# The order of the first loads and of the second pair's preparation in a fused Mamba-2 and feed-forward kernel

## Chip, cores and metric

The kernel runs on one core of one Trainium2 chip. The metric is the device time of one execution in microseconds (us), the median over runs. Matrix products run on TensorE (PE in the profile), elementwise work on VectorE (DVE), ScalarE (ACT) and GpSimd (POOL); SyncE (SP) issues most of the transfers, GpSimd those of the weights, and all transfers are carried out by 16 DMA engines.

## What is computed

The first part is a linear-recurrence attention (Mamba-2 SSD) over 4 batches, 8 heads and 768 positions with head size 32 and state size 16; its result, laid out as 3072 tokens of 256 features, goes through a feed-forward layer with 2048 hidden units and a squared ReLU.

```python
# x (4,8,768,32)  a (4,8,768)  B, C (4,8,768,16)  w_in (256,2048)  w_out (2048,256), all float32
log_a = np.log(np.clip(a, 1e-06, 1.0))
for c in range(nc):                         # chunks of 32 positions, state (N x D) per head
    cum = np.cumsum(la, axis=-1)
    L = np.exp(cum[..., :, None] - cum[..., None, :]) * causal
    CB = np.einsum('bhin,bhjn->bhij', Cc, Bc)
    y_intra = np.einsum('bhij,bhjd->bhid', CB * L, xc)
    y_inter = np.einsum('bhin,bhnd->bhid', Cc, state) * np.exp(cum)[..., None]
    y[:, :, sl] = y_intra + y_inter
    state = decay_full * state + np.sum(Bx * decay_from_j, axis=2)
x2 = y.transpose(0, 2, 1, 3).reshape(3072, 256)
h = np.maximum(x2 @ w_in, 0.0)
out = (h * h) @ w_out
```

## The kernel before

**Tiling.** The 768 positions of a batch are cut into three stretches of 256, which gives 12 pairs (batch, stretch), `PAIRS`, numbered k = 0 to 11 with the four batches first. Each pair is one block of 256 tokens for the feed-forward layer. The kernel uses a chunk length of its own, two chunks u of 128 positions in each pair, and two positions (r = 0, 1) in a partition.

**Attention of one pair.** `ph_load(k)` issues three transfers on SP (for pair 0, B goes by ScalarE's queue): C and B of 128 KB each, in pieces of 128 bytes, and x of 256 KB, in pieces of 256 bytes. With `gate=`, an engine first writes one element of each buffer, so that the transfer can't be issued before that engine has come to this place. `prep_c` scales C by the cumulative decay `P_sb` (tile cz for the first four pairs), `prep_b` casts B to bfloat16 (Bb), `prep_x` multiplies x by the inverse decay `Pinv` (xs). `ph_tr` transposes Bb and cz on TensorE (six matmuls into tile tr), `ph_bct` copies them out of PSUM on VectorE (bct). `ph_mt` multiplies C with B (mt), `ph_mask` applies the causal mask in four parts (mts), `ph_u` forms the state contribution U from Bb and xs, `ph_s` the state (S, z) and `ph_y` the result Y, which is copied to `T[k]`, the transposed input of the feed-forward layer. For pair 0, half of T is copied by ScalarE and half by VectorE.

**Feed-forward layer.** A step is a block and one of eight parts f of 256 hidden units. `mm1` multiplies `w_in_b` with T (tile hps) and ScalarE applies the ReLU (hb); `square` squares it on VectorE (h), but for the first step on GpSimd; `mm2` multiplies with `w_out_b` four steps later (ops). `finish_block` writes the block out.

**Weights.** They are loaded and cast to bfloat16 by GpSimd's queue in slices of 256 KB (as written): `load_wi(f0, f1)` and `load_wo(f0, f1)`, with f counting groups of 128 hidden units. There are four slices of each, and a small `tensor_copy` to the tile `touch` ahead of some of them reads a tile that another engine has to have written; it holds GpSimd, and so the issue behind it, until then. Before, the first slice wi(0:4) waits in this way for the decay input `a_nat` (line 450), and wi(4:8) for Bb of pair 0 (line 491).

**Order.** All engines work through their instructions in the order of the program; the scheduling is by hand (`manual_schedule`). Lines 445 to 523 are the prologue written out one by one: pair 0, and pair 1 up to its transposes. `warm(n, cols)` puts n matmuls on dummy data into TensorE's queue (tile dps). From line 525 on, a list of steps and a table `todo` say what is issued at each step: before the change, step 0 issues xs of pair 1 and the gated loads of pair 2 (`second_x`), step 3 U of pair 1, step 4 its Y and the `late_loads` (three slices of weights behind a touch of pair 1's state, then the gated loads of pair 3). Pair 2 has its transposes at step 9, U at 12 and Y at 14. GpSimd makes cz of pair 2 at step 6 and its xs at step 7. From pair 4 on, a DMA transpose takes the place of the transposes on TensorE.

Of the kernel before, what the change touches and what calls it, by code (L numbers as in the profile page):

```python
# [16 lines left out]
def _fap(base: bass.AP, offset_elems: int, free_dims):  # L17

    ap0 = list(base.ap)[0]
    return bass.AP(tensor=base.tensor, offset=base.offset + offset_elems,  # L20
                   ap=[list(ap0)] + [list(d) for d in free_dims])


def _dap(base: bass.AP, offset_elems: int, dims):

    return bass.AP(tensor=base.tensor, offset=base.offset + offset_elems,
                   ap=[list(d) for d in dims])
# [3 lines left out]
def kernel(  # L31
# [14 lines left out]
    nc = tc.nc  # L46
# [43 lines left out]
    a_nat = const.tile([96, 256], FP32, name="a_nat")  # L90
    a_cl = const.tile([96, 256], FP32, name="a_cl")
    dum = const.tile([128, 256], BF16, name="dum")
    touch = const.tile([128, 1], FP32, name="touch")
# [3 lines left out]
    P_sb = const.tile([128, 2, 96], FP32, name="P_sb")  # L97
# [32 lines left out]
    def load_wi(f0, f1):  # L130
        nc.gpsimd.dma_start(
            out=w_in_b[:, :, f0 * 128:f1 * 128],
            in_=_dap(moe_w_in, f0 * 128, [[2048, 128], [128 * 2048, 2], [1, (f1 - f0) * 128]]))

    def load_wo(f0, f1):
        nc.gpsimd.dma_start(  # L136
            out=w_out_b[:, f0:f1, :],
            in_=moe_w_out[f0 * 128:f1 * 128, :].rearrange("(f p) d -> p f d", p=128))


    live = {}

    def prep_c(k, eng):
        b, j = PAIRS[k]
        if k >= KDT:
            for r in range(2):
                eng.tensor_tensor(  # L147
                    out=_fap(bc[k % 3], r * 384 + 128, [[144, 2], [32, 4], [1, 16]]),
                    in0=_fap(loaded[k]["C"], r * 16, [[128, 2], [32, 4], [1, 16]]),
                    in1=_fap(P_sb, r * 96 + b * 24 + j, [[12, 2], [3, 4], [0, 16]]), op=ALU.mult)  # L150
            return
        czk = cz[k % 3]
        eng.tensor_tensor(
            out=_fap(czk, 0, [[240, 2], [32, 8], [1, 16]]),
            in0=_fap(loaded[k]["C"], 0, [[16, 2], [32, 8], [1, 16]]),
            in1=_fap(P_sb, b * 24 + j, [[96, 2], [3, 8], [0, 16]]), op=ALU.mult)
        live.setdefault(k, {})["cz"] = czk

    def prep_b(k, eng):
        if k >= KDT:  # L160
            Bb = bc[k % 3][:, :, 0, :]
        else:
            Bb = prep.tile([128, 2, 128], BF16, tag="Bb", name=f"Bb{k}")
        for r in range(2):
            bo = _fap(Bb, r * (384 if k >= KDT else 128), [[16, 2], [32, 4], [1, 16]])
            bi = _fap(loaded[k]["B"], r * 16, [[128, 2], [32, 4], [1, 16]])
            if eng is nc.scalar:
                eng.copy(out=bo, in_=bi)
            else:
                eng.tensor_copy(out=bo, in_=bi)  # L170
        live.setdefault(k, {})["Bb"] = Bb

    def prep_x(k, eng):
        b, j = PAIRS[k]
        xs = prep.tile([128, 2, 256], BF16, tag="xs", name=f"xs{k}")
        eng.tensor_tensor(  # L176
            out=_fap(xs, 0, [[256, 2], [32, 8], [1, 32]]),
            in0=_fap(loaded[k]["x"], 0, [[32, 2], [64, 8], [1, 32]]),
            in1=_fap(Pinv, b * 24 + j, [[96, 2], [3, 8], [0, 32]]), op=ALU.mult)
        live.setdefault(k, {})["xs"] = xs  # L180
# [14 lines left out]
    def ph_tr(k, copy=True):  # L195
        v = live[k]
        pool, tag = (ps_o, "ops") if k < 2 else (ps_s, "A")
        tr = pool.tile([128, 2, 3, 128], BF16, tag=tag, name=f"tr{k}",
                       padded_shape=[128, 2, 4, 128] if k < 2 else [128, 4, 4, 128])
        for r in range(2):  # L200
            nc.tensor.transpose(tr[:, r, 0, :], v["Bb"][:, r, :], eye_b)
            for g in range(2):
                nc.tensor.transpose(tr[:, r, 1 + g, :], v["cz"][:, r, 112 * g:112 * g + 128], eye_b)  # L203
        v["tr"] = tr
        if copy:
            ph_bct(k)

    def ph_bct(k):
        bct = big.tile([128, 2, 3, 128], BF16, tag="bct", name=f"bct{k}")
        nc.vector.tensor_copy(out=bct, in_=live[k]["tr"])  # L210
        live[k]["bct"] = bct
# [17 lines left out]
    def ph_mask(k, q, src=None):  # L229
        v = live[k]  # L230
        nc.vector.tensor_tensor(  # L231
            out=v["mts"][:, q], in0=v["mt"][q // 2][:, q % 2] if src is None else src,
            in1=_fap(cb, 128, [[128, 2], [0, 2], [1, 128]]), op=ALU.mult)
# [210 lines left out]
    with tc.manual_schedule():  # L444
# [2 lines left out]
        ph_load(0, "C")  # L447
        ph_load(0, "B", nc.scalar)
        nc.gpsimd.dma_start(out=cb, in_=cb_d.ap())
        nc.gpsimd.tensor_copy(out=touch[0:96], in_=a_nat[:, 0:1])  # L450
        load_wi(0, 4)

        nc.vector.memset(dum, 0.0)  # L453
        nc.vector.memset(zer, 0.0)
# [8 lines left out]
        def idle_tile():  # L463
            idle.append(ps_o.tile([128, 256], FP32, tag="ops", name=f"dps{len(idle)}", padded_shape=[128, 512]))
# [3 lines left out]
        def warm(n, cols=256):  # L468
            for _ in range(n):
                nc.tensor.matmul(idle[-1][:, 0:cols], dum[:, 0:128], dum[:, 0:cols],  # L470
                                 start=True, stop=True, skip_group_check=True)
# [16 lines left out]
        nc.scalar.copy(out=Ptot, in_=pps)  # L488
        prep_c(0, nc.vector)
        nc.vector.reciprocal(out=_fap(Pinv, 0, [[96, 2], [3, 32]]), in_=_fap(P_sb, 0, [[96, 2], [3, 32]]))  # L490
        nc.gpsimd.tensor_copy(out=touch, in_=live[0]["Bb"][:, 1, 0:1])
        load_wi(4, 8)
        prep_x(0, nc.gpsimd)
        warm(2, 128)
        ph_tr(0)
        warm(8, 128)
# [2 lines left out]
        mtc = big.tile([128, 2, 2, 2, 128], BF16, tag="mtc", name="mtc", bufs=1)  # L499
        for i in (1, 0):  # L500
            nc.scalar.copy(out=mtc[:, i], in_=live[0]["mt"][1][:, i])
        ph_mask(0, 0)
        nc.gpsimd.tensor_copy(out=touch, in_=live[0]["mts"][:, 0, 0, 0, 0:1])
        load_wo(0, 4)
        prep_b(1, nc.gpsimd)
        load_wo(4, 8)
        load_wi(8, 12)
        nc.gpsimd.tensor_tensor(out=Pown, in0=_fap(Ptot, 0, [[1, 24], [0, 4]]),
                                in1=_fap(cb, 384, [[0, 24], [1, 4]]), op=ALU.mult)
        warm(4, 128)  # L510
        ph_u(0)
        warm(12, 128)
        ph_mask(0, 1)
        ph_mask(0, 3, mtc[:, 1])
        ph_mask(0, 2, mtc[:, 0])
        ph_s(0, (0,))
        prep_c(1, nc.vector)
        ph_y(0)
        ph_tr(1, copy=False)
        idle_tile()  # L520
        warm(5, 128)
        ph_bct(1)
        ph_s(0, (1,), "z")

        steps = ([(0, f) for f in range(4)] + [(1, f) for f in range(4)]
# [4 lines left out]
        def at(s, fn, *args):  # L530
            todo.setdefault(max(s, 0), []).append((fn, args))
# [1 line left out]
        def recip_rest(j):  # L533
            nc.vector.reciprocal(out=_fap(Pinv, j, [[96, 2], [3, 32]]), in_=_fap(P_sb, j, [[96, 2], [3, 32]]))

        def second_x():
            prep_x(1, nc.gpsimd)
            ph_load(2, gate=nc.gpsimd)

        def late_loads():  # L540
# [3 lines left out]
            load_wo(12, 16)  # L544
            ph_load(3, gate=nc.gpsimd)

        at(0, second_x)
        at(4, late_loads)
        at(8, ph_s, 0, (1,), "S")
        for j, s in ((1, 13), (2, 20)):  # L550
# [84 lines left out]
```

## Time and profile before

| what | value |
|---|---|
| median of 6 runs | 118.9 us (117.41 to 120.22) |
| profiled execution | 119.15 us, span 117.3 us |
| granted TensorE clock | 1.0 in the whole span |
| busy in the span | PE 110.6, DVE 87.7, ACT 73.3, POOL 36.9 us |
| transfers | 10.77 MB read, 3.15 MB written |
| U of pair 2 starts on TensorE | 26.40 us |
| x of pair 2: issued, landed | 14.83, 25.15 us |

Times in views of the profile are counted from the start of the span. A matmul counts as busy from its start to its modelled end, so busy time of TensorE says little of how well it is used, and its warm matmuls count too. A wait is put down to what came last before the waiting instruction started. For a transfer there is the time of issue, how long the issue took on its queue, and the time from issue to landing; the busy share of the 16 DMA engines in a stretch is given as a sum that can be over 1 where packets overlap.

### The profile page before, as it was taken

The page shows a single profiled execution, that of the slowest core. Times are in us where ns is not written, and L with a number is a line of the kernel's source. Part 1 is how long each engine was busy: PE and PEld are TensorE (multiplying, and loading weights), DVE is VectorE, ACT ScalarE, POOL GpSimd, SP SyncE. Part 2 cuts the span into 40 slices and gives each one's busy share as a digit, 9 for nine tenths or more (in the row PEclk, how much of TensorE's full clock was granted, in tenths as well). Part 3 has the DMA queues.
Part 4 walks back from the last instruction along what each step waited for, and adds up shares of the span by engine and source line. Part 5 has one row for each costly group of instructions (what it writes and reads, how often), then busy time and mean ns, then how long its engine had stood idle before and what let it go on. Part 6 is the DMA issues. An engine that isn't in the chain of part 4 may idle for free.

```text
span 117.3 us, 4063 instructions
## 1 busy us (share of the span) xinstructions
PE 110.6 (94%) x1678; PEld 90.8 (77%) x1678; DVE 87.7 (75%) x200; ACT 73.3 (63%) x137; POOL 36.9 (31%) x75
## 2 busy tenths in 40 slices
PE   6989889969999999999999999999999999999980
PEld 4757568647787787788788787887887887888970
DVE  6477847599999699998697794995975966935440
ACT  4144747647588566586586577586675866866830
POOL 3368983039880430620530332234300000000000
PEclk9999999999999999999999999999999999999999
DMA  3999999999747915906918918949150020020202
GB/s 78 226 115 219 171 177 159 186 169 213 140 144 175 206 36 143 198 0 153 166 24 177 151 60 171 99 125 209 31 156 8 3 89 6 0 89 0 94 1 89
DMA packets 49923, 13.66 MB, mean 116 GB/s; under 512 B 44304, under 2 KB 48992, under 8 KB 49904
## 3 DMA queue, kind: packets, MB, share of 16 engines
q1 hardware_dynamic: 45360, 10.85, 48.2%
q0 software_dynamic: 3248, 2.20, 13.8%
q10 hardware_dynamic: 1296, 0.35, 1.5%
q8 instruction: 13, 0.21, 0.7%
q14 instruction: 6, 0.05, 0.1%
HBM read 10.77 MB, written 3.15 MB: 119 GB/s over the span
## 4 chain that ended last, share of the span: by engine, by line
PE 78%; DMA 9%; DVE 5%; POOL 2%; issue 1%; ACT 1%; DVEq 0%; POOLq 0%
PE hps L370 31%; PE ops L399 30%; DMA x_nat<-in_x_dram 9%; PE dps L470 5%; PE mt L220 3%; PE Y L304 3%; DVE mts L231 2%; POOL xs L176 2%; DVE h L380 2%; PE Y L333 1%; PE U L249 1%; PE ops_r L399 1%; PE ops L415 1%; DVE S L290 1%; PE ops_r L415 1%
## 5 line engine op out<-in xcount | busy, mean ns | idle before, releaser
L374 ACT ACTIVATE hb<-hps 128x512 bf16<-128x512 f32 x96 | 57.4, 599 | 30.4 <-PE hps L370 27.2
L370 PE MATMUL hps<-T,w_in_b 128*128 128x256 bf16 x384 | 57.4, 273 | 0.1
L399 PE MATMUL ops<-w_out_b,h 128*128 128x256 bf16 x360 | 55.0, 273 | 0.8 <-DMA w_out_b<-in_moe_w_out_dram 0.6
L380 DVE TENSOR_TENSOR h<-hb 128x512 bf16<-128x512 bf16 x95 | 43.3, 479 | 11.8 <-ACT hb L374 11.4
L370 PEld LDWEIGHTS <-w_in_b 128*128 128x128 bf16 x384 | 37.2, 98 | 4.8 <-issue 0.5
L399 PEld LDWEIGHTS <-h 128*128 128x128 bf16 x376 | 34.5, 98 | 7.2 <-issue 1.8
L231 DVE TENSOR_TENSOR mts<-mt,cb 128x512 bf16<-128x512 f32 x46 | 30.3, 684 | 8.4 <-PE mt L220 8.4
L176 POOL TENSOR_TENSOR xs<-x_nat,Pinv 128x512 bf16<-128x512 f32 x12 | 13.0, 1081 | 14.1 <-DMA x_nat<-in_x_dram 13.3
L147 POOL TENSOR_TENSOR bc<-C_nat,P_sb 128x128 bf16<-128x128 f32 x16 | 7.0, 456 | 25.3 <-DMA C_nat<-in_C_dram 25.3
L470 PE MATMUL dps<-dum 128*128 128x128 bf16 (+1 forms) x66 | 8.5, 280 | 1.1 <-DVE dum L453 1.1
L470 PEld LDWEIGHTS <-dum 128*128 128x128 bf16 x66 | 5.8, 115 | 2.4 <-DVE dum L453 1.1
L290 DVE TENSOR_TENSOR S<-z,Pown 128x256 bf16<-128x256 f32 x16 | 6.9, 430 | 0.5
L359 ACT CAST T<-Y 128x512 bf16<-128x512 f32 x11 | 6.4, 585 | 0.9 <-PE Y L337 0.9
L437 ACT COPY osb<-ops 128x512 f32<-128x512 f32 x11 | 6.4, 581 | 0.3 <-PE ops L399 0.3
L220 PE MATMUL mt<-bct 32*64 32x256 bf16 x192 | 5.4, 280 | 0.2 <-DVE bct L210 0.2
L170 POOL CAST bc<-B_nat 128x128 bf16<-128x128 f32 x16 | 5.1, 349 | 1.3 <-DMA B_nat<-in_B_dram 1.3
L304 PE MATMUL Y<-mts,xs 64*32 64x128 bf16 x384 | 5.0, 219 | 0.0
L220 PEld LDWEIGHTS <-bct 32*64 32x64 bf16 x192 | 2.0, 102 | 2.9 <-issue 1.9
L304 PEld LDWEIGHTS <-xs 64*32 64x32 bf16 x384 | 2.9, 91 | 1.6 <-issue 0.6
L283 DVE SCALAR_TENSOR_TENSOR z<-z,Ptot,U 128x64 f32<-128x64 f32 x12 | 3.3, 274 | 0.5 <-PE U L249 0.5
L210 DVE COPY bct<-tr 128x768 bf16<-128x768 bf16 x4 | 2.2, 558 | 1.5 <-PE tr L203 1.2
L136 POOL DMA_DIRECT2D w_out_b<-in_moe_w_out_dram x4 | 3.2, 790 | 0.3 <-issue 0.3
(61 smaller groups left out, 52.3 us busy)
## 6 DMA issues: line engine op xcount, KB each, us to landing
x_nat<-in_x_dram SPq DMA_DIRECT2D x12, 256.0 KB, 4.6
out_dram<-osb SPq DMA_DIRECT2D x7, 256.0 KB, 2.2
C_nat<-in_C_dram SPq DMA_DIRECT2D x12, 128.0 KB, 3.0
B_nat<-in_B_dram SPq DMA_DIRECT2D x11, 128.0 KB, 3.4
w_in_b<-in_moe_w_in_dram POOLq DMA_DIRECT2D x4, 256.0 KB, 6.0
w_out_b<-in_moe_w_out_dram POOLq DMA_DIRECT2D x4, 256.0 KB, 5.5
out_dram<-osb SPq DMA_DIRECT2D x8, 128.0 KB, 1.8
B_nat<-in_B_dram ACTq DMA_DIRECT2D x1, 128.0 KB, 3.7
```

Of the source, the lines that this page charges most:

```text
L147: eng.tensor_tensor(out=_fap(bc[k % 3], r * 384 + 128, [[144, 2], [32, 4], [1, 16]]), in0=_fap(loaded[k]["C"], r * 16, [[128, 2], [32, 4], ...
L176: eng.tensor_tensor(out=_fap(xs, 0, [[256, 2], [32, 8], [1, 32]]), in0=_fap(loaded[k]["x"], 0, [[32, 2], [64, 8], [1, 32]]), in1=_fap(Pinv ...
L220: nc.tensor.matmul(mt[q // 2][64 * u:64 * u + 64, q % 2, r, :, :], bct[32 * q:32 * q + 32, r, 0, u * 64:u * 64 + 64], _fap(bct[32 * q:32 * ...
L231: nc.vector.tensor_tensor(out=v["mts"][:, q], in0=v["mt"][q // 2][:, q % 2] if src is None else src, in1=_fap(cb, 128, [[128, 2], [0, 2], ...
L290: nc.vector.tensor_tensor(out=S_n.rearrange("p (g q d) -> p g q d", g=2, q=4), in0=_fap(z, 0, [[32, 2], [0, 4], [1, 32]]), in1=_fap(Pown, ...
L304: nc.tensor.matmul(Y[u][32 * q:32 * q + 32, g, :], v["xs"][64 * u:64 * u + 64, r, h * 32:h * 32 + 32], v["mts"][64 * u:64 * u + 64, q, r, ...
L359: nc.scalar.copy(out=_fap(T[k], 0, [[64, 2], [128, 4], [1, 64]]), in_=_fap(Y[0], 0, [[512, 2], [64, 4], [1, 64]]))
L370: nc.tensor.matmul(hps[:, i, :], w_in_b[:, g, f * 128:(f + 1) * 128], T[blk][:, g].rearrange("p r u t -> p (r u t)"), start=(g == 0), stop ...
L374: nc.scalar.activation(out=hb, in_=hps, func=AF.Relu)
L380: (nc.gpsimd if blk == 0 and fp == 0 else nc.vector).tensor_tensor(out=h2, in0=hb, in1=hb, op=ALU.mult)
L399: nc.tensor.matmul(o[c], h2[:, i, r * 128:(r + 1) * 128], w_out_b[:, f, c * 128:(c + 1) * 128] if len(o) > 1 else w_out_b[:, f, :], start= ...
L470: nc.tensor.matmul(idle[-1][:, 0:cols], dum[:, 0:128], dum[:, 0:cols], start=True, stop=True, skip_group_check=True)
```

## The change

Six edits in the prologue and one in the step list; no operation of the reference's computation is added or left out.

- The touch of `a_nat` and wi(0:4) are taken from GpSimd's queue at the start. wi(0:4) is now issued right ahead of wi(4:8), behind one touch that reads `P_sb`.
- cz of pair 1 is made by GpSimd, behind xs of pair 0, and no longer by VectorE.
- Bb of pair 1 is cast by ScalarE, behind its two mtc copies, and no longer by GpSimd.
- xs of pair 1 stands on GpSimd between wo(0:4) and wo(4:8), and no longer at step 0.
- The transposes of pair 1 and their copy by VectorE stand ahead of Y of pair 0.
- The warm matmuls behind U of pair 0 are six in place of twelve, with two new ones behind the transposes.
- Step 0 issues only the gated loads of pair 2 (`third_load`).

```diff
         nc.gpsimd.dma_start(out=cb, in_=cb_d.ap())
-        nc.gpsimd.tensor_copy(out=touch[0:96], in_=a_nat[:, 0:1])
-        load_wi(0, 4)
...
-        nc.gpsimd.tensor_copy(out=touch, in_=live[0]["Bb"][:, 1, 0:1])
+        nc.gpsimd.tensor_copy(out=touch, in_=P_sb[:, 0, 0:1])
+        load_wi(0, 4)
         load_wi(4, 8)
         prep_x(0, nc.gpsimd)
+        prep_c(1, nc.gpsimd)
...
+        prep_b(1, nc.scalar)
         ph_mask(0, 0)
         nc.gpsimd.tensor_copy(out=touch, in_=live[0]["mts"][:, 0, 0, 0, 0:1])
         load_wo(0, 4)
-        prep_b(1, nc.gpsimd)
+        prep_x(1, nc.gpsimd)
         load_wo(4, 8)
...
         ph_u(0)
-        warm(12, 128)
+        warm(6, 128)
...
         ph_s(0, (0,))
-        prep_c(1, nc.vector)
+        ph_tr(1)
+        idle_tile()
+        warm(2, 128)
         ph_y(0)
-        ph_tr(1, copy=False)
-        idle_tile()
         warm(5, 128)
-        ph_bct(1)
         ph_s(0, (1,), "z")
...
-        def second_x():
-            prep_x(1, nc.gpsimd)
+        def third_load():
             ph_load(2, gate=nc.gpsimd)
...
-        at(0, second_x)
+        at(0, third_load)
```

## The prediction

> **What bounds the kernel now.** I read the waits of TensorE first, then the chain that ended last, then TensorE's timeline up to the first long wait, then the DMA issues one by one. Names: pair k's loads are C_k, B_k, x_k; slices of the weights are wi(0:4), wo(0:4) and so on; U(k), Y(k), T(k) are the stages of pair k, xs(k), Bb(k), cz(k) its prepared operands.
>
> TensorE's waits (engine, line, what it waited for; us in total, times, longest):
>
> ```profile
> PE U L249 <- POOL xs L176: 1.3, 2, 1.1
> PE ops L399 <- DMA w_out_b<-in_moe_w_out_dram: 0.6, 1, 0.6
> PE mt L220 <- DVE bct L210: 0.2, 1, 0.2
> ```
>
> The chain that ended last (start, us, what):
>
> ```profile
> 14.83 10.32 DMA x_nat<-in_x_dram
> 25.16 0.02 issue
> 25.18 0.02 POOLq L176
> 25.20 0.09 issue
> 25.29 1.07 POOL xs L176
> 26.36 0.04 issue
> 26.40 0.25 PE U L249 x16
> ```
>
> From 26.40 the chain is TensorE, except for 5.7 us of VectorE work around 40 to 45, in which TensorE itself waits 0.2 us. So the end is the start of U(2) plus 90.9 us (117.3 - 26.4), and U(2) starts when x_2 has landed (25.15) and GpSimd has made xs(2): landing plus 1.25. TensorE is there earlier:
>
> ```profile
> 24.67 0.60 PE L370 MATMUL hps<-T,w_in_b 128*128 128x256 bf16 x4
> 26.40 0.25 PE L249 MATMUL U<-xs,Bb 64*32 64x64 bf16 x16 [1.13 <-POOL xs L176]
> ```
>
> It arrives at 25.27 and idles 1.13 us. That is the reading on which all the rest stands: **whatever the change does ahead of 25 us, a TensorE that comes up to 1.13 us later costs nothing, and one that comes earlier gains nothing, unless x_2's landing moves.**
>
> x_2 is a matter of the DMA engines. Its issue on SP and that of the last weight slice on GpSimd, and what two single issues took to land:
>
> ```profile
> 14.83 2.70 SPq L125 DMA_DIRECT2D x_nat<-in_x_dram  x1
> 17.11 0.78 POOL L136 DMA_DIRECT2D w_out_b<-in_moe_w_out_dram  x1
> x_nat<-in_x_dram SPq DMA_DIRECT2D x1, 256.0 KB, 10.3
> w_out_b<-in_moe_w_out_dram POOLq DMA_DIRECT2D x1, 256.0 KB, 7.9
> ```
>
> Issue plus time to landing, one after another, gives this order of landings: wi(0:4) 9.85, B_1 10.3, x_1 11.2, wi(4:8) 12.65, wo(0:4) 14.9, wo(4:8) 16.2, wi(8:12) 17.7, C_2 18.25, B_2 18.9, wo(8:12) 20.4, wi(12:16) 22.5, wo(12:16) 25.0, x_2 25.15, C_3 25.7. It is one saturated server; x_2 lands when all that was asked for before it is done. The stages show where it was not saturated (last three columns: granted clock, DMA share, GB/s):
>
> ```profile
> 4.00:6.00 2.00, 2.00 (x13) 1.46 (x10) 1.11 (x5) 0.48 (x3) 0.76 (x2) 1.00 1.02 202
> 6.00:7.50 1.50, 1.29 (x17) 0.88 (x16) 1.32 (x3) 0.31 (x3) 0.85 (x2) 1.00 0.85 75
> 7.50:11.30 3.80, 3.61 (x108) 2.73 (x109) 2.72 (x6) 1.97 (x5) 3.07 (x7) 1.00 1.20 204
> ```
>
> **GpSimd's order, part by part.** Removed: the early touch of a_nat (0.30) with wi(0:4) (0.72) at 3.81; prep_b(1) (0.53, and 0.29 of waiting for B_1). Added: wi(0:4) later, cz(1). The new touch waits for P_sb, which ScalarE ends at 5.84, so it starts near 5.9 and not at 6.37. From a touch to the next issue takes 0.46 (6.37 to 6.83), or 0.24 (3.81 to 4.05): wi(0:4) is issued at 6.15 to 6.35, 2.1 to 2.3 later than now; wi(4:8) 0.71 on, at 6.85 to 7.05 (now 6.83); xs(0) 0.82 on, at 7.7 to 7.9 (now 7.65). cz(1) follows: other cz on GpSimd took 0.63 and 0.82 against 0.42 on VectorE; nearest in load is 0.63, with 0.82 as the end. wo(0:4) comes 0.53 after that (as 8.73 to 9.26 now): 9.9 to 10.3, take 10.1 (now 9.26). Then 0.81 for it and 1.08 for xs(1), which is now ahead of wo(4:8): 12.0 (now 10.84), and wi(8:12) 12.75 (now 11.58). The gate memsets of pair 2's loads come 4.35 - 0.53 - 0.29 = 3.53 after wo(0:4): 13.65, between 13.45 and 13.85 (now 13.61). So the three weight issues are 0.8 to 1.2 late, pair 2's loads are not, and the square of block 0 behind them (13.74 now) isn't either.
>
> The Trainium skill (GPSIMD Engine Reference, 4.1 Engine selection) speaks against this move: a two-input elementwise operation on GpSimd is to be some two times slower than on VectorE. By it, cz(1) would be 0.84, and the gates 0.2 later than by the row of 0.63; the rows here say 1.5 to 1.95 times.
>
> **TensorE's front.** U(0) ends at 9.04 now, at 9.17 with xs(0) 0.13 later. Six warm matmuls in place of twelve take 0.39 of 0.78: 9.56. The transposes of pair 1 need cz(1) (7.8 + 1.08 + 0.63 = 9.5, at worst 9.8) and Bb(1), which ScalarE now casts after its two mtc copies (end 9.09; two casts 0.50: 9.6). They take 0.58: 10.2; two warm 0.13, Y's first part 0.22, four warm 0.33, its second part 0.35: 11.2, now 10.71. Sf and zc, queued on ScalarE behind the casts, are 0.4 later (9.6 to 9.9) and still ahead of Y. The copy bct(1) on VectorE (0.56, 10.2 to 10.8) stands before its half of T(0) and is over in time. T(0) comes 0.55 after Y: 11.75; the first W_in matmul now starts at 11.56, held by the transposes and five warm that no longer stand between. Net +0.2 (0 to +0.5).
>
> It also needs wi(0:4). Issued at 6.25 and landing after its own 5.8: 12.05. The ends are the shortest and longest time to landing of a GpSimd slice, 4.8 and 7.9: 11.05 to 14.15. I take 12.05, since the queue ahead of it is what it was: TensorE is 0.5 late. wo(0:4) issued 0.85 later would land at 15.7 by its 5.6; its user starts at 14.93 now, so up to 0.8 late in all (not added: both are waits of the same engine). TensorE then arrives at U(2) at 26.1 at the latest, hidden by the 1.13; without that cover it would cost the 0.8. Removing prep_c from VectorE (0.42) and four warm (0.26) is hidden the same way.
>
> **x_2.** Gain: the dip at 6.0 to 7.5, at 0.85 of a share where the next stage has 1.20, is 0.44 us of lost service ((1.20 - 0.85) x 1.5 / 1.20), by bytes 0.95 ((204 - 75) x 1.5 / 204). It fell where wi(0:4) met B_1 and x_1. Issued after them, it leaves SP's loads alone, which in the first stage ran at 202 GB/s. Loss: wo(0:4) is 0.85 late (0.65 to 1.05), which counts as far as the server runs dry near 12.6. Ends: 0.95 earlier to 1.05 later; I take 0.3 earlier: the smaller gain, 0.44, less a sixth of the 0.85, since the slices before it keep the server busy up to about 12.6 and most of the delay is hidden behind them. x_2 lands at 24.85, U(2) starts at 26.1, and TensorE is there just in time. **Sum: 0.3 us off the profiled 119.15 (span 117.3 and 1.85 around it): 118.85.** That execution is 0.25 above the median, so against 118.9 it is **118.6**, with 117.9 to 119.9 as this case's own range.
>
> The Trainium skill (DMA: Bandwidth & Descriptors, Issuing engines are not separate DMA queues) says that transfers of all queues run on the same 16 engines and interleave. By it alone, order is no gain at all and the sum is 0; the dip to 75 GB/s above is what the rule does not foresee.
>
> **Rivals.**
> 1. *x_2 slips ahead of wo(12:16).* It would land 1.0 (x_3 behind B_3: 27.4 - 26.4) after wi(12:16): 23.5. xs(2) ends before TensorE arrives, and the whole 1.13 is won, if wi(0:4) is not late either; with 0.1 of the wait for wo(0:4) (VectorE's and GpSimd's squares hold it to 14.84) it is 1.2 to 1.3: **117.6**. For it: SP's issue now ends 0.36 before that slice's (17.53 against 17.89), and the two land together. Against: the slices land late in front. 0.22.
> 2. *x_2 falls behind wo(12:16).* SP's issue of x_2 takes 2.70 us because C_2 and B_2 are still queued; these now stand behind wo(4:8) and wi(8:12) issued 1.2 later. If that holds SP beyond the 0.36, x_2 is served last: wo(12:16) at 25.0 plus 0.65, plus 1.0 for itself: 26.65, 1.5 later. **120.4**, slower. It decides from a landing after 26.35. Against: the stream is no longer as a whole. 0.22.
> 3. *The first weights come too late.* At 7.9 to landing wi(0:4) is there at 14.15; TensorE is 2.6 late, 1.13 hidden: **120.4**. It decides from 13.9. Against: nothing is queued on GpSimd ahead of it. 0.14.
> 4. *Pair 1's loads don't come earlier* (their issues on SP, 3.6 to 6.0, are not moved). B_1 at 10.3 holds ScalarE's casts, so the transposes end 1.2 later, TensorE is 1.4 late, 0.3 shows: **119.2**, no change. It is held within the chance of the forecast.
>
> **How the numbers follow.** 1% (1.2 us) is about what a measurement of this kernel can tell. Forecast with rival 4: 0.42. Rival 1 gives faster 0.22, rivals 2 and 3 slower 0.36. The range takes in the rivals' times, 117.4 to 120.5.
>
> **What would show it.** Right: wi(0:4) issued near 6.2, x_1 landed by 9.5, GpSimd's cz(1) near 9, gate memsets within 0.3 of 13.6, U(2) within 0.7 of 26.1 and still behind xs(2). A U(2) with no wait, or with TensorE as the late one, shows rival 1 or 3; x_2 landing more than 0.5 after wo(12:16) shows rival 2. Wrong altogether: a chain in which x_2 is not, or a granted clock below 1.00 where warm matmuls went.

## The result, and the profile after

The changed kernel takes 119.79 us in the median of 34 runs, against 118.97 us of 71 runs of the kernel before on the same chips. The ratio is 1.0078 with a 95% interval of 1.0059 to 1.0097: it is **slower by 0.9 us**, where 0.3 us faster was predicted. (Ratios here and below leave out executions more than 1.5% above the fastest of the same kernel; medians do not.) The profiled execution took 119.45 us, with a span of 117.7 us, against 119.15 and 117.3 us.

**TensorE's waits.** Engine, line, what it waited for; us in total, times, longest. After:

```profile
PE Y L304 <- DVE mts L231: 1.1, 1, 1.1
PE U L249 <- DVE mts L231: 0.6, 2, 0.4
PE U L249 <- POOL xs L176: 0.4, 1, 0.4
PE hps L370 <- DVE z L281: 0.3, 1, 0.3
```

The 1.1 us in front of U for xs, on which the prediction stood, are gone (the 0.4 left are those of U(0)). In their place Y of pair 0 waits 1.1 us for VectorE's masks.

**Where the masks are held.** VectorE's timeline around the two masks that read `mtc` (start, us, engine, line, operation), before and then after:

```profile
9.18 0.75 DVE L231 TENSOR_TENSOR mts<-mtc,cb 128x512 bf16<-128x512 bf16 x2
9.85 0.42 DVE L153 TENSOR_TENSOR cz<-C_nat,P_sb 128x256 bf16<-128x256 f32 x1
```

```profile
7.47 1.29 DVE L231 TENSOR_TENSOR mts<-mt,cb 128x512 bf16<-128x512 f32 x2 [0.54 <-PE mt L220]
8.67 2.73 DVE L231 TENSOR_TENSOR mts<-mtc,cb 128x512 bf16<-128x512 bf16 x2
11.33 0.55 DVE L210 COPY bct<-tr 128x768 bf16<-128x768 bf16 x1
```

The same two instructions take 2.73 us in place of 0.75 (1.53 and 1.28 us, which overlap by 0.08). GpSimd in that stretch, before and then after:

```profile
9.26 0.81 POOL L136 DMA_DIRECT2D w_out_b<-in_moe_w_out_dram  x1 [0.27 <-issue]
10.36 0.53 POOL L170 CAST Bb<-B_nat 128x128 bf16<-128x128 f32 x2 [0.29 <-DMA B_nat<-in_B_dram]
```

```profile
7.33 1.08 POOL L176 TENSOR_TENSOR xs<-x_nat,Pinv 128x512 bf16<-128x512 f32 x1
8.36 0.64 POOL L153 TENSOR_TENSOR cz<-C_nat,P_sb 128x256 bf16<-128x256 f32 x1
8.94 0.18 POOL L504 CAST touch<-mts 128x1 f32<-128x1 bf16 x1
9.07 0.81 POOL L136 DMA_DIRECT2D w_out_b<-in_moe_w_out_dram  x1
9.90 1.21 POOL L176 TENSOR_TENSOR xs<-x_nat,Pinv 128x512 bf16<-128x512 f32 x1
```

cz(1) and xs(1), both moved here by the change, stand beside the masks. The second mask ends at 11.40, which is 0.29 us after xs(1) (9.90 + 1.21 = 11.11). The two masks ahead of them, which read `mt` in PSUM, run beside xs(0) (7.33 to 8.41) and are not held: 1.29 us for the two, as before the change. TensorE pays for the hold, as its timeline shows:

```profile
11.46 0.41 PE L304 MATMUL Y<-mts,xs 64*32 64x128 bf16 x30 [1.13 <-DVE mts L231]
11.80 0.45 PE L468 MATMUL dps<-dum 128*128 128x128 bf16 x5
12.55 0.60 PE L370 MATMUL hps<-T,w_in_b 128*128 128x256 bf16 x4 [0.30 <-DVE z L281]
```

The first W_in matmul starts at 12.55, 1.14 us after the 11.41 of before.

**x of pair 2.** It is issued at 14.11 and lands 9.0 us later at 23.11, ahead of two of the late weight slices (landed 21.95, 23.76, 25.25) and 2.0 us earlier than before. But U(2) does not start earlier. The timelines of VectorE, GpSimd and TensorE:

```profile
23.72 1.03 DVE L290 TENSOR_TENSOR S<-z,Pown 128x256 bf16<-128x256 f32 x1
24.68 0.68 DVE L231 TENSOR_TENSOR mts<-mt,cb 128x512 bf16<-128x512 f32 x1
```

```profile
23.27 1.20 POOL L176 TENSOR_TENSOR xs<-x_nat,Pinv 128x512 bf16<-128x512 f32 x1 [3.46 <-DMA x_nat<-in_x_dram]
```

```profile
26.43 0.26 PE L249 MATMUL U<-xs,Bb 64*32 64x64 bf16 x16 [0.42 <-DVE mts L231]
```

xs(2) is ready at 24.47. TensorE, late from the front, comes to U(2) at 26.01 and then waits 0.42 us for masks on VectorE, where the state S of pair 1 took 1.03 us beside xs(2) in place of 0.42 before. U(2) starts at 26.43, against 26.40. The chain that ended last shows the exchange, shares of the span by engine (after):

```profile
PE 77%; DVE 18%; issue 1%; ACT 1%; DVEq 0%
```

Before, transfers had 9% of this chain and VectorE 5%; now no transfer is in it.

### The profile page after: what moved, and what is told of

Its sections match the earlier page's. It is cut to its first block, busy times and chain, and to the rows that moved or that the text cites. A ratio compares the mean times of both kernels' runs of the same rounds, so it can differ in the third digit from the quotient of the medians.

```text
span 117.7 us, 4053 instructions
## 1 busy us (share of the span) xinstructions
PE 110.1 (94%) x1674; PEld 90.2 (77%) x1674; DVE 87.5 (74%) x199; ACT 73.7 (63%) x139; POOL 36.8 (31%) x73
## 3 DMA queue, kind: packets, MB, share of 16 engines
HBM read 10.77 MB, written 3.15 MB: 118 GB/s over the span
## 4 chain that ended last, share of the span: by engine, by line
PE 77%; DVE 18%; issue 1%; ACT 1%; DVEq 0%
PE hps L370 30%; PE ops L399 30%; DVE mts L231 11%; DVE h L380 4%; PE mt L220 4%; PE Y L304 3%; PE dps L468 3%; PE Y L333 2%; PE U L249 1%; DVE S L290 1%; PE ops_r L399 1%; PE tr L201 1%; PE ops L415 1%; PE tr L203 1%; PE ops_r L415 1%
## 5 line engine op out<-in xcount | busy, mean ns | idle before, releaser
L380 DVE TENSOR_TENSOR h<-hb 128x512 bf16<-128x512 bf16 x95 | 40.7, 452 | 11.3 <-ACT hb L374 11.2
L176 POOL TENSOR_TENSOR xs<-x_nat,Pinv 128x512 bf16<-128x512 f32 x12 | 13.7, 1139 | 9.4 <-DMA x_nat<-in_x_dram 5.9
L468 PE MATMUL dps<-dum 128*128 128x128 bf16 (+1 forms) x62 | 7.9, 273 | 1.1 <-DVE dum L451 1.1
L290 DVE TENSOR_TENSOR S<-z,Pown 128x256 bf16<-128x256 f32 x16 | 7.4, 462 | 0.5
L170 POOL CAST bc<-B_nat 128x128 bf16<-128x128 f32 x16 | 4.4, 303 | 1.4 <-DMA B_nat<-in_B_dram 1.1
```

The costliest lines, as they stand in the source:

```text
L176: eng.tensor_tensor(out=_fap(xs, 0, [[256, 2], [32, 8], [1, 32]]), in0=_fap(loaded[k]["x"], 0, [[32, 2], [64, 8], [1, 32]]), in1=_fap(Pinv ...
L290: nc.vector.tensor_tensor(out=S_n.rearrange("p (g q d) -> p g q d", g=2, q=4), in0=_fap(z, 0, [[32, 2], [0, 4], [1, 32]]), in1=_fap(Pown, ...
L380: (nc.gpsimd if blk == 0 and fp == 0 else nc.vector).tensor_tensor(out=h2, in0=hb, in1=hb, op=ALU.mult)
```

## Experiments

There are fifteen runs, each beside the kernel before. The columns are from the profiled execution of each (start of the first W_in matmul, landing of x of pair 2, start of U(2), span, us); the ratio is against the kernel before on the same chip. Landings are the time of issue plus the time to landing, which the profile gives to 0.1 us. The profiled executions of runs 1, 9 and 14 were the longest of their kernel (121.43, 121.98 and 121.89 us against medians of 120.35, 120.23 and 120.59), so their spans say more than the usual loss.

| run | first W_in | x_2 landed | U(2) | span | ratio, 95% interval |
|---|---|---|---|---|---|
| before | 11.41 | 25.15 | 26.40 | 117.3 | 1 |
| after | 12.55 | 23.11 | 26.43 | 117.7 | 1.0078, 1.0059 to 1.0097 |
| 1 masks in PSUM | 11.48 | 25.81 | 27.08 | 119.5 | 1.0112, 1.0054 to 1.0170 |
| 2 xs(1) late | 11.73 | 25.53 | 26.76 | 117.7 | 1.0006, 0.9978 to 1.0035 |
| 3 cz(1) on VectorE | 14.63 | 20.76 | 28.41 | 119.3 | 1.0169, 1.0124 to 1.0214 |
| 4 load order alone | 11.37 | 25.45 | 26.84 | 117.5 | 1.0021, 0.9989 to 1.0053 |
| 5 before, late touch | 11.99 | 23.72 | 25.93 | 116.7 | 0.9917, 0.9885 to 0.9949 |
| 6 masks in PSUM, late touch | 11.60 | 26.02 | 27.26 | 117.9 | 0.9978, 0.9934 to 1.0021 |
| 7 load order and xs(1) early | 12.45 | 23.52 | 25.89 | 116.9 | 1.0027, 0.9988 to 1.0065 |
| 8 after, 20 warm | 12.89 | 23.54 | 26.78 | 117.8 | 1.0034, 1.0002 to 1.0066 |
| 9 after again | 11.91 | 26.47 | 27.97 | 120.1 | 1.0086, 1.0048 to 1.0124 |
| 10 load order, late touch | 11.47 | 20.45 | 25.00 | 115.9 | 0.9937, 0.9905 to 0.9968 |
| 11 xs(1) late, late touch | 11.50 | 20.83 | 26.08 | 117.1 | 0.9952, 0.9916 to 0.9988 |
| 12 xs(2) behind S | 12.91 | 23.48 | 27.69 | 118.3 | 1.0121, 1.0080 to 1.0162 |
| 13 after, late touch | 12.95 | 23.61 | 26.80 | 117.8 | 0.9975, 0.9919 to 1.0031 |
| 14 after, early touch | 12.73 | 26.26 | 28.51 | 120.1 | 1.0148, 1.0084 to 1.0211 |
| 15 after, 20 warm, late touch | 12.52 | 20.51 | 25.84 | 116.8 | 1.0009, 0.9978 to 1.0039 |

"Late touch" is the small copy on GpSimd ahead of the last three weight slices, when it reads T of pair 1 and not its state.

**The theories.** The first was: the masks on `mtc`, held by GpSimd's work on SBUF, make TensorE late, and this is the loss. Its first rival: the loss comes through x of pair 2 and the transfers around it. The second: another of the moved steps, cz(1) on GpSimd or the load order, costs it.

### 1. The masks read PSUM

```diff
-        ph_mask(0, 3, mtc[:, 1])
-        ph_mask(0, 2, mtc[:, 0])
+        ph_mask(0, 3)
+        ph_mask(0, 2)
```

This is the changed kernel with the last two masks reading `mt` in PSUM.

> The changed kernel, but the masks (0,3) and (0,2) of pair 0 read their product from PSUM and not from the bfloat16 copy mtc in SBUF (ScalarE still makes the copy, nothing reads it). GpSimd's work is as in the changed kernel. Theory 'collision' (a VectorE operation with both inputs in SBUF is held up while GpSimd works on SBUF data; the two masks took 2.73 us where they took 0.75): the two masks take 2 x 0.68 = 1.3 us, the 1.1 us wait of Y on TensorE goes, the first W_in matmul starts 1.0 to 1.3 us earlier, U of pair 2 near 25.2 to 25.5, and the time is 0.985 to 0.995 of before. Rival 'order' (the transposes and the copy ahead of Y, and the later weights, are what costs): the masks are no shorter than 2 us or their end does not matter, and the time stays at 1.005 to 1.01 of before.

The four masks now run in 2.48 us without a hold, and the first W_in matmul starts at 11.48, as before the change. In this execution xs(1) started only at 10.77, behind its load, when the masks were over. Run 6, with the same masks, is the closer test: its GpSimd makes cz(1), issues the slice (9.45 to 10.26) and starts xs(1) (10.28) at the same places as in run 13, whose masks on `mtc` take 2.73 us, and its masks are free (0.68 us each). So the hold belongs to two operands in SBUF on VectorE against GpSimd, and it made the whole of the front's 1.1 us. It isn't a matter of bfloat16, in which the masks on `mtc` are the quicker ones (0.41 us): the state S reads float32 and is held as well. But the time did not get better: 1.0112, where 0.985 to 0.995 was expected. With the front on time the late slices are issued at 15.69 in place of 16.75, and x of pair 2 falls behind all three of them (landed 25.81). TensorE's timeline:

```profile
27.08 0.25 PE L249 MATMUL U<-xs,Bb 64*32 64x64 bf16 x16 [1.92 <-POOL xs L176]
```

What the front gained is given back as a wait of 1.92 us. The first theory is half right: the hold is there, its removal alone wins nothing.

### 2. xs of pair 1 back at step 0

```diff
         load_wo(0, 4)
-        prep_x(1, nc.gpsimd)
         load_wo(4, 8)
...
         def third_load():
+            prep_x(1, nc.gpsimd)
             ph_load(2, gate=nc.gpsimd)
```

> The changed kernel, but xs of pair 1 is made at step 0 again, ahead of the gated loads of pair 2, as in the kernel before. Theory 'collision': only cz of pair 1 still stands beside the masks; the first mask on mtc is held (1.0 to 1.5 us as in the changed kernel), the second is free again (0.4) unless issuing weight slices holds it too; the first W_in matmul starts 0.8 to 1.2 us earlier than in the changed kernel, and the time is 0.99 to 1.0 of before. Rival 'order': no gain, 1.005 to 1.01.

The masks take 0.75 us again and the ratio is 1.0006. So xs(1) at its new place is the edit that holds them (cz(1) still stands ahead of them here), and without it the loss is gone, although x of pair 2 lands as late as 25.53. A wait of 1.29 us ahead of the first W_out matmul (it starts at 15.98; wo(0:4) landed at 15.93) shows that the rest of the change has a price of its own, which was hidden under x of pair 2.

### 3. cz of pair 1 on VectorE

```diff
         prep_x(0, nc.gpsimd)
-        prep_c(1, nc.gpsimd)
...
         ph_s(0, (0,))
+        prep_c(1, nc.vector)
         ph_tr(1)
```

> The changed kernel, but cz of pair 1 is made by VectorE again, ahead of the transposes of pair 1. Theory 'collision': the masks meet no GpSimd operation (xs of pair 1 starts behind wo(0:4), about 0.6 earlier than now, near 9.3, when the masks end), they take 0.75 to 1.2 together, cz itself may wait on xs of pair 1; the time is 0.988 to 1.0 of before. Rival 'order': 1.005 to 1.01, since the transposes are still ahead of Y and wait for VectorE.

The worst of all, 1.0169 where 0.988 to 1.0 was expected: xs(1) was still beside the masks. The second of them was held (1.95 us), and cz(1), queued behind them on VectorE, came only at 11.42. VectorE's timeline, then TensorE's at the transposes:

```profile
9.21 2.28 DVE L231 TENSOR_TENSOR mts<-mtc,cb 128x512 bf16<-128x512 bf16 x2
11.42 0.41 DVE L153 TENSOR_TENSOR cz<-C_nat,P_sb 128x256 bf16<-128x256 f32 x1
```

```profile
11.89 0.29 PE L203 MATMUL tr<-cb,cz 128*128 128x128 bf16 x2 [2.13 <-DVE cz L153]
```

TensorE stood 2.13 us, and the granted clock fell behind that. In the windows of this run (us; busy time and count of PE, PEld, DVE, ACT, POOL; granted clock, DMA share, GB/s):

```profile
10.00:12.00 2.00, 0.11 (x2) 0.12 (x3) 1.83 (x2) 0.00 (x0) 1.98 (x4) 1.00 1.15 149
12.00:14.00 2.00, 2.00 (x53) 1.23 (x52) 0.56 (x1) 0.00 (x1) 1.11 (x5) 0.56 1.21 157
14.00:16.00 2.00, 1.98 (x26) 1.00 (x26) 0.56 (x2) 0.69 (x2) 0.00 (x0) 0.59 1.23 129
```

So the move of cz(1) to GpSimd is no loss within this change: it keeps cz(1) out of the queue behind the held masks.

### 4 and 7. Single edits on the kernel before

Run 4 is the kernel before with the new order of the first weight slices alone; run 7 has this order and xs(1) behind wo(0:4).

```diff
-        nc.gpsimd.tensor_copy(out=touch[0:96], in_=a_nat[:, 0:1])
-        load_wi(0, 4)
...
-        nc.gpsimd.tensor_copy(out=touch, in_=live[0]["Bb"][:, 1, 0:1])
+        nc.gpsimd.tensor_copy(out=touch, in_=P_sb[:, 0, 0:1])
+        load_wi(0, 4)
         load_wi(4, 8)
```

> The kernel before with only the order of the loads changed: wi(0:4) goes behind the touch of P_sb, with wi(4:8). Theory 'collision': the loads are not what costs: pair 1's loads land 2 to 3 us earlier (C_1 near 6.8, x_1 near 8.6), the masks take 0.75 as before, x of pair 2 lands 0.5 to 2 us earlier than 25.1, and the time is 0.99 to 1.0 of before. Rival 'late weights': the first weight slices are what costs, TensorE waits for wi or wo ahead of 16 us, and the time is 1.003 to 1.01.

> The kernel before with the new order of the loads and with xs of pair 1 directly behind wo(0:4) on GpSimd; cz of pair 1 stays on VectorE, Bb of pair 1 on GpSimd (now behind xs), the transposes stay behind Y. Theory 'collision': the second of the two masks on mtc, or cz behind it on VectorE, is held until xs of pair 1 ends (near 11.0), T of pair 0 is 0.8 to 1.2 us late, the first W_in matmul near 12.3 to 12.7; the late slices follow, x_2 lands ahead of 24.5, and the time is 1.002 to 1.01 of before. Rival 'only the transposes ahead of Y make the masks matter': masks 0.75 to 0.85 together, 0.998 to 1.004 as with the loads alone.

The load order brings x of pair 1 in at 9.40 in place of 11.2, and yet x of pair 2 lands at 25.45 (before 25.15): the smoother front gains nothing where the prediction, and this run's expectation, counted a gain. Run 7 has the hold without any of the transposes' moves (masks 2.29 us, Y waits 0.82 us), which repeats what run 2 says of the hold from the other side. It does not repeat the loss: the ratio is 1.0027, not to be told from the 1.0021 of run 4. Its profiled execution had x of pair 2 early and was the shortest of its kernel (118.66 against a median of 119.19 us).

### 5 and 6. The late touch

```diff
-            nc.gpsimd.tensor_copy(out=touch, in_=live[1]["S"][1][:, 0:1])
+            nc.gpsimd.tensor_copy(out=touch, in_=T[1][:, 0, 0, 0, 0:1])
...
-        at(4, late_loads)
+        at(5, late_loads)
```

Run 5 puts this on the kernel before, run 6 on run 1.

> The kernel before, with one edit: the three late weight slices (wo(8:12), wi(12:16), wo(12:16)) wait on GpSimd for T of pair 1 and not for its first state, about 1.5 us later than before, so that SP's issue of x of pair 2 ends well ahead of theirs. Theory 'late slices displace x_2' (in the changed kernel the slices are 1.1 us late because the front is late, and x_2 landed at 23.1 and not 25.1): x_2 lands near 23 to 23.7, U of pair 2 starts at 25.3 to 25.6 and TensorE hardly waits for it; 0.988 to 0.996 of before. Rival 'x_2 is bound by the sum of the traffic': it still lands after 24.7, the time is 0.997 to 1.004.

> The changed kernel with the masks of pair 0 read from PSUM (no collision) and the late weight slices held until T of pair 1. Theory 'collision plus late slices': the front is as early as in the run with PSUM masks alone (first W_in matmul near 11.5), x_2 lands near 23 to 24 and not 25.8, U of pair 2 at 25.0 to 25.6, 0.985 to 0.995 of before. Rival 'order of the transposes costs by itself': 1.005 or more, as with the PSUM masks alone.

Run 5, the smallest edit of all, is the best kernel here: 0.9917. Its late slices go out at 17.82, x of pair 2 lands at 23.72, and U(2) starts when TensorE comes (0.17 us of waiting; TensorE's timeline):

```profile
25.93 0.25 PE L249 MATMUL U<-xs,Bb 64*32 64x64 bf16 x16 [0.17 <-DVE mts L231]
```

So the wait for x of pair 2 that bounded the kernel before is removed by holding back the slices, and this needs none of the change. Run 6 missed its expectation. Its issue of x of pair 2 took 4.26 us and ended at 18.58, the last slice's at 19.55, and x of pair 2 was still last (26.02) in the profiled execution; its executions spread from 117.45 to 122.73 us.

### 8. More warm matmuls in the gap

```diff
         if k == 0:
-            warm(4, 128)
+            warm(20, 128)
```

> The changed kernel with 20 warm matmuls in place of 4 between the two parts of Y of pair 0, which fill the wait of 1.1 us for the masks. Theory 'collision': TensorE has no wait there but Y starts no sooner (near 11.45), the undisturbed runs stay at 1.004 to 1.01 of before. Rival 'clock' (the wait lowers TensorE's granted clock in part of the runs, and that is what is measured): granted clocks of 0.98 become rarer than 10 in 35, and the ratio falls to 0.998 to 1.003.

No execution of 12 had a granted clock below 0.995; of 35 executions of the changed kernel whose clock is on record, twelve were at 0.982 to 0.986 and took 119.9 to 121.9 us. So the low clock goes with the wait. The ratio of 1.0034 lies between the two expectations, and its interval overlaps that of the changed kernel: what the clock is worth is not settled by this run.

### 9 to 12. The changed kernel again, and three versions beside it

> The changed kernel itself, on the chip of the three others, so that they are compared with it as well as with the kernel before. Expected as before: masks on mtc 2.7 us long, first W_in matmul near 12.5, x of pair 2 landed 23.1 to 23.6, U of pair 2 at 26.4 to 26.8 behind the masks (0.4 us of waiting). Ratio 1.003 to 1.010.

The ratio came again (1.0086), the course of the profiled execution did not. The masks were held for 0.9 us less. VectorE's timeline in this run:

```profile
8.94 1.83 DVE L231 TENSOR_TENSOR mts<-mtc,cb 128x512 bf16<-128x512 bf16 x2
```

The touch of the masks and the late slices on GpSimd's timeline, and U(2) on TensorE's:

```profile
9.20 0.40 POOL L504 CAST touch<-mts 128x1 f32<-128x1 bf16 x1
16.11 0.81 POOL L136 DMA_DIRECT2D w_out_b<-in_moe_w_out_dram  x1
16.92 0.71 POOL L131 DMA_DIRECT2D w_in_b<-in_moe_w_in_dram  x1
17.61 0.78 POOL L136 DMA_DIRECT2D w_out_b<-in_moe_w_out_dram  x1
```

```profile
27.97 0.31 PE L249 MATMUL U<-xs,Bb 64*32 64x64 bf16 x16 [2.65 <-POOL xs L176]
```

Y waited only 0.22 us, the late slices went out 0.64 us earlier than in the first profile (16.11 against 16.75) while x of pair 2 was issued 0.56 us later (14.67 against 14.11), it came last of all (26.47), and U(2) waited 2.65 us. This gave the next theory: the changed kernel has **two courses**. Either the front is held and x of pair 2 comes early, for nobody; or the front is hardly held, the slices go out earlier, and x of pair 2 is late. Which one it is goes with the order of the touch and the first mask: the touch took 0.18 us and the mask 1.53 in the first profile, 0.40 and 0.62 in this one. The first profile cost 0.3 us (119.45 against 119.15), the second 1.57 us at U(2) and a lower clock behind the wait (0.51 in the window from 28 to 30 us).

Run 10 is run 4 with the late touch:

> The kernel before with the two edits that touch no VectorE or GpSimd arithmetic: the new order of the first weight slices, and the touch ahead of the last three slices moved from the state of pair 1 (step 4) to T of pair 1 (step 5). Theory (what is to be won here is x of pair 2 ahead of the last slices, with a front that is not held): first W_in matmul near 11.4, masks on mtc 0.9 us or less, x of pair 2 landed 23 to 24, U of pair 2 at 25.1 to 25.9 with 0.3 us of waiting or less; ratio 0.985 to 0.993. Rival (the new order makes the queues such that x of pair 2 is late in spite of the later touch, as in the run with masks in PSUM and a late touch, where it landed at 26.02): U of pair 2 at 26.8 or later, ratio 0.996 to 1.003.

0.9937, with x of pair 2 at 20.45 (23 to 24 was expected) and the earliest U(2) of all, on TensorE's timeline without a wait:

```profile
25.00 0.25 PE L249 MATMUL U<-xs,Bb 64*32 64x64 bf16 x16
```

The ratio is just above the expected interval (0.985 to 0.993) and no better than run 5's (the intervals overlap; they ran on different chips). Run 11 is run 2 with the late touch:

> The changed kernel with xs of pair 1 back at step 0 and the touch ahead of the last three slices moved to T of pair 1 (step 5). Theory: without xs beside the masks nothing is held (first W_in matmul near 11.7, masks 0.75 us each as in the run with only xs moved back), x of pair 2 lands at 23.5 to 24 and U of pair 2 starts at 25.6 to 26.0; the wait of 1.3 us for the first W_out slice may stay, as it lies in front; ratio 0.990 to 0.998. Rival (the rest of the change costs the same whether x of pair 2 is early or not): 0.999 to 1.004.

0.9952, as expected, with x of pair 2 earlier than expected (20.83): most of the change is harmless once xs(1) stands elsewhere and the slices wait. The 1.30 us ahead of the first W_out matmul stayed, and U(2) is 1.08 us behind run 10's. Run 12 took up the second hold, S beside xs(2):

```diff
+        def behind_s(k):
+            nc.gpsimd.tensor_copy(out=touch, in_=live[1]["S"][2][:, 0:1])
+            prep_x(k, nc.gpsimd)
...
-                at(7, prep_x, k, nc.gpsimd)
+                at(11, behind_s, k)
```

> The changed kernel with xs of every later pair moved from step 7 to step 11, behind a touch that reads the last part of the state S of pair 1, so that xs of pair 2 can't run beside VectorE's S. Theory (the second hold costs the 0.4 us that U of pair 2 waits for the masks, and VectorE's later backlog): S back at 0.42 us, U of pair 2 at 26.0 to 26.2 if xs is ready by then (touch, then 1.2 us), ratio 0.003 to 0.005 below that of the changed kernel. Rival (the hold of S is covered, or xs behind S is itself late): U of pair 2 at 26.4 or later, ratio within 0.002 of the changed kernel's.

S took 0.42 us again, so xs(2) had held it. But the gain did not come: 1.0121. U(2) still waited 0.50 us for masks, since the square h beside the later xs(2) now took 0.96 in place of 0.41 us. The hold moved to the next instruction on VectorE with two operands in SBUF. In this execution the granted clock also fell to 0.50 after the wait of 1.12 us in the front, so the price of the second hold by itself stays open.

### 13 to 15. x of pair 2 fixed early and fixed late

Run 13 is the changed kernel with the late touch. Run 14 is the opposite: the touch reads T of pair 0 at step 3. Run 15 is run 13 with the 20 warm matmuls of run 8.

```diff
-            nc.gpsimd.tensor_copy(out=touch, in_=live[1]["S"][1][:, 0:1])
+            nc.gpsimd.tensor_copy(out=touch, in_=T[0][:, 0, 0, 0, 0:1])
...
-        at(4, late_loads)
+        at(3, late_loads)
```

> The changed kernel with one edit: the touch ahead of the last three weight slices reads T of pair 1 at step 5, not its state at step 4. x of pair 2 is then to land early (20.8 to 23.6) in all executions, while the masks on mtc are held as before and TensorE waits for them. Theory A (the 0.9 us of the changed kernel are the mean over executions in which x of pair 2 lands early and only the hold is left, 0.3 us, and executions in which it lands after 26 and 1.5 us are lost): ratio 0.999 to 1.004, U of pair 2 at 26.0 to 26.5. Theory B (the loss is the held masks, the held S and the lower clock behind them, with x of pair 2 early or late): ratio 1.006 to 1.010, as the changed kernel.

> The changed kernel with the opposite edit: the touch ahead of the last three weight slices reads T of pair 0 at step 3, so that they are issued near 15.0 to 15.5 and x of pair 2 is behind them in all executions (landing 25.5 to 26.5). Theory A: U of pair 2 at 26.9 to 28.0 behind xs, ratio 1.010 to 1.016, above that of the changed kernel. Theory B: 1.006 to 1.010, as the changed kernel.

> The changed kernel with the late touch (T of pair 1, step 5) and 20 warm matmuls in place of 4 between the two parts of Y of pair 0, so that TensorE doesn't stand still while the masks are held. With x of pair 2 early in all executions and no execution with a granted clock below 0.995, only the hold of the masks in front is left. Theory A: ratio 0.997 to 1.002, and below that of the run with the late touch alone by the share of its executions that have a lower clock. Theory B: 1.002 to 1.006, as with the warm matmuls alone (1.0034).

Late by design costs 1.0148, 1.8 us, but not through x of pair 2 alone. It landed at 26.26 and xs(2) was ready at 27.48; U(2) started later still, at 28.51, because B of pair 2, landed at 24.03 behind the same slices, had made TensorE's transposes wait 2.0 us, and the first W_in matmul had waited 0.93 us for its weights. Early by design and with the warm matmuls nothing is lost that can be measured: 1.0009, with no wait at U(2) on TensorE's timeline:

```profile
25.84 0.25 PE L249 MATMUL U<-xs,Bb 64*32 64x64 bf16 x16
```

The changed kernel (1.0078 and 1.0086) stands between these two, as theory A wants, but runs 14 and 15 differ by two edits, and each of the two taken alone is unclear. With the warm matmuls alone (run 8) 1.0034 was measured, and the interval overlaps both others. With the late touch alone (run 13) the ratio of 0.9975 rests on four of twelve executions (117.6 to 119.1 us), while the median is 119.62 against 118.74 us, a loss of 0.9 us as theory B wants. Four of the others had a clock of 0.984 to 0.986, but four had 0.995 to 1.000 and took 119.6 to 120.2 us. The profiled execution was one of those: x of pair 2 landed at 23.61, xs(2) again ran beside S (1.10 us), and U(2) waited 0.50 us for the masks and started at 26.80. In run 15 x of pair 2 came at 20.51, S was held too (1.95 us, from 20.34), but so early that nobody waited. So with x of pair 2 early by 1.5 us TensorE meets the second hold, and with x early by 4.6 us it does not.

**What is settled and what is not.** Shown: xs(1) at its new place holds the masks, and moving it back takes away both the hold and the loss (run 2: 1.0006 against 1.0078). The hold alone is not the loss: without it run 1 still lost 1.1%, and run 7 has it at 1.0027. Pair 2's loads behind the late slices cost 1.8 us (run 14); ahead of them, and with the gap in front filled, the change costs nothing (run 15). Argued: how the hold comes to 0.9 us, by x of pair 2 that is late in one course, by the second hold in the other, and by the lower clock. Left open: what the late touch and the filled gap are worth singly, in which share of its executions the changed kernel takes which course, since only two of them were profiled, and when exactly GpSimd takes hold (below).

## Why the prediction was wrong

**What bounds the kernel: right.** The end is U(2) plus 90.9 us. Span less U(2) is 91.3 after, and 90.8, 90.9, 91.0 and 91.0 in runs 5, 10, 11 and 15. It is longer where the clock fell behind U(2) (92.1 in run 9). The 1.13 us at U(2) were a real cover: with the first W_in matmul 1.14 us late, TensorE came to U(2) 0.74 us late (26.01 against 25.27), which by itself cost nothing.

**GpSimd's order: right, its times somewhat late.** wi(0:4) was issued at 5.81 in the profile after (predicted 6.15 to 6.35; 6.08 in run 9), cz(1) took 0.64 (0.63), x of pair 1 landed at 8.58 (by 9.5). The gate memsets came at 12.88 (13.45 to 13.85), because GpSimd's touch started at 5.44 and not near 5.9, and because wo(0:4) followed cz(1) without the 0.53 us that were counted between them; in run 9 they came at 13.44. The weights were not late as rival 3 has it: wi(0:4), issued at 6.08, landed at 10.68 in run 9, against 12.05 in the sum, and only run 14 shows TensorE waiting for it (0.93 us). For wo(0:4) 15.7 was predicted; it landed at 15.9 in run 2 and at 15.7 in run 11, where its user started 1.05 and 0.84 us late (up to 0.8 predicted), and at 14.7 in the profile after.

**TensorE's front: the step that failed.** The sum gave +0.2 us for the first W_in matmul, 0 to +0.5, and 1.14 was measured. The working itself was sound: without the hold, runs 1, 6 and 11 have +0.07, +0.19 and +0.09. The omitted term is VectorE's masks. The prediction counted what moved off VectorE as relief and costed xs(1) and cz(1) on GpSimd's own queue, but put what stands beside them on VectorE at nothing; the masks then took 2.0 us more (2.73 against 0.75). The line of before that should have been asked is that of the masks: two operands in SBUF, 0.41 us each, over at 9.94 while GpSimd was issuing a transfer, with its next operation, the cast of Bb, only at 10.36. The Trainium skill has the rule (SBUF — State Buffer, section "SBUF: two separate sides"): a VectorE operation with two SBUF inputs and a GpSimd operation that reads SBUF exclude each other, and whichever starts first blocks the other. The 2.73 us here agree that they exclude each other; which of the two comes first does not follow from the recorded starts (run 7, below).

**x of pair 2: the second step that failed.** The gain of 0.3 us from the load order isn't there: 25.45 in run 4 against 25.15. The dip in the second stage was real, but service won at 6 to 8 us did not bring forward a transfer that is issued at 14 us. Nor is it one server that takes transfers in order: in the profile before, all three late slices were issued behind x of pair 2 (15.61 to 17.11 against 14.83) and landed ahead of it. What the landing goes with is the gap between the issue of x of pair 2 and that of the late slices (last section). The change alters it at both ends: x is issued when GpSimd reaches the gates, and the slices when TensorE's front is through, since their touch waits for a state that comes behind Y. The prediction held the slices' issue to be fixed; it lay at 16.75, 16.11, 15.69 and 17.82 us in the profile after and in runs 9, 1 and 5, and x of pair 2 landed at 23.11, 26.47, 25.81 and 23.72.

**The rivals.** Rival 1 happened in the first profile, as far as the landing goes (predicted 23.5, measured 23.11), but not its time: it took TensorE to be early. Rival 2 happened in the second: it named a landing after 26.35 and 1.5 us, and 26.47 and 1.57 us at U(2) were measured. The prediction took one or the other to come true; that one kernel would take both courses was not among its cases. The reason given for rival 2, that SP's issue is long because two loads are still queued, is not shown: in the profile before, x of pair 1 was issued in 0.81 us with C and B of pair 1 still under way. Rival 4 was wrong: pair 1's loads came earlier. That 119.79 us lies within the range of 117.9 to 119.9 is luck: the range was drawn from the ends of x of pair 2, and the hold of the masks is in none of them.

**The clock.** "A granted clock below 1.00 where warm matmuls went" was named as what would make the prediction wrong. It came in part of the executions (in run 12's profile after a wait of 1.12 us), and it lifts the median: the 12 executions of the changed kernel with a lower clock have a median of 120.65 us, the 23 others one of 119.49. A loss stays without it: 0.5 us against the 118.97 of before, and 0.9 us in run 9 (nine executions, 120.08 against 119.18).

## What to carry to other kernels

An operation moved to GpSimd has to be costed on VectorE too: look up which VectorE instructions with two operands in SBUF will stand beside it, and what is queued behind them. Slack at a later meeting point hides a late front, but a late front also shifts whatever is gated by it, here the weight slices; follow each gate before calling a delay hidden. If a transfer is the bound, hold back what competes with it: one edited touch (run 5) gained 1 us where seven edits lost 0.8 in the median.

## What was not expected of the hardware

- **The hold can begin before GpSimd's operation shows.** In run 7 the second mask began near 9.34 and ended at 11.30, though xs(1) is recorded from 9.93 to 11.01, behind an issue on the same queue (GpSimd's timeline of run 7; its spans are rough):

```profile
9.10 0.81 POOL L136 DMA_DIRECT2D w_out_b<-in_moe_w_out_dram  x1 [0.23 <-issue]
9.93 1.08 POOL L176 TENSOR_TENSOR xs<-x_nat,Pinv 128x512 bf16<-128x512 f32 x1
```

  In run 11 the state S began at 20.57 and took 1.96 us, with xs(2) recorded from 21.14. In run 4, with a cast next on GpSimd behind the same issue (9.05 to 9.86, then the cast), the two masks took 0.84 us and were over at 9.80.
- **Which side is held is a race.** Seven profiles have the change's order on GpSimd and the masks on `mtc`. Where the touch ahead of wo(0:4) took 0.18 to 0.19 us, the first mask on `mtc` took 1.52 to 1.53 us, and the second ended 0.3 us after xs(1) (after, runs 8, 12, 13). Where the touch took 0.38 to 0.40 us, the first mask took 0.55 to 0.62 us, the second ended before xs(1), and xs(1) itself took 1.30 us (runs 9, 14, 15). What GpSimd takes hold of, and when, was not tried further.
- **A short wait can halve the clock.** It fell to 0.56 after 2.13 us without matmuls (run 3) and to 0.50 after 1.12 us (run 12), and stayed at 1.00 after 1.13 us in the profile after and after 2.05 us in run 14. The Trainium skill (TensorE: Matmul & The Clock Gate, Part 1: The HAM clock gate) speaks of an idle window of some 3.4 us; the drops here came after less. With 20 warm matmuls in the gap, no execution of 24 (runs 8 and 15) was below 0.995.
- **Service goes nearly by when an issue ends.** x of pair 2 landed at 20.4 to 20.9 us where its issue on SP ended 0.7 us or more ahead of the first late slice's (runs 3, 10, 11, 15), at 25.1 to 26.5 where it ended behind the second slice's (before, runs 1, 2, 4, 9, 14), and at 23.1 to 23.8 in between (after, runs 5, 7, 8, 12, 13). Run 6 is an exception, at 26.02.
